# Gated linear recurrence with a maxout feed-forward: a new order of all steps and PSUM rooms, 45 words in column quarters, and the second group's decay sum by an adding transfer

## The chip, the cores and the metric

One core of one Trainium2 chip. The metric is the device time in microseconds of one execution. The kernel before took 555.67 us (median of 3 runs, 555.03 to 556.41).

## What is computed

The reference, cut to what matters (B, H, S, D = 4, 8, 768, 48; 3072 tokens, d_model 384, d_ff 768):

```python
mag = np.sqrt(a_re * a_re + a_im * a_im)
scale = np.minimum(mag, 0.999) / (mag + 1e-06)
a_re_n, a_im_n = (a_re * scale, a_im * scale)
for t in range(S):
    new_re = ar * S_re - ai * S_im          # ar, ai: a_re_n, a_im_n at t
    new_im = ar * S_im + ai * S_re
    kv = np.einsum('bhd,bhe->bhde', k[:, :, t], v[:, :, t])
    S_re, S_im = (new_re + kv, new_im)
    y[:, :, t] = np.einsum('bhd,bhde->bhe', q[:, :, t], S_re)
x = y.transpose(0, 2, 1, 3).reshape(B * S, H * D)
h = np.maximum(np.maximum(x @ w1, x @ w2), x @ w3)
return (h @ w_out).astype(np.float32)
```

A complex decay per head and channel multiplies a state in each of the 768 steps, the state takes k times v and is read by q; the result of all heads goes through three products, their maximum, and one more product. The weights arrive as float64.

## The kernel before, in words

The recurrence is made of blocks of 128 steps. A **group** (number 0 to 11 after the colon of a word) holds one block for two batch entries, x and y; two runs of six groups cover four entries. The decay is taken apart into a size (as a sum of logarithms, tile Ln) and an angle (running sums of turns, cs, then sines). q and k are scaled and turned by those, transposed (tp), and multiplied for scores within a block (A and B, picked into atm by masks); across blocks a state g is carried (dk, and h-steps on it). `y` adds scores times v and q times the state. The feed-forward for a group of 256 tokens: `U` multiplies by w2 and w3 after w1 was subtracted from them (so the third branch folds into wp, from T, M and W steps at the start), the u-steps take the maximum, and P1 to P7 with S1 to S4, r- and o-steps are one level of Strassen's scheme for the last product; Px and Py add the third branch.

Every step is a **word** such as `U01:3` or `Kcx:5`, and `SCHEDULE` lists all words in one order. `run` turns a word into instructions; class `Bound` ties each instruction to the one before it on its engine, so the engines (PE, DVE, ACT, POOL, and SP for loads and stores) each follow the list in their own order and wait only by semaphores. Line 107 is the helper through which all of them go, so every row of the profile carries it, and rows are told apart by their tiles. `SLOTS` says which of four PSUM rooms of two banks each a word's result takes; a room is free when its readers are done. `OTHER` names the words that run on the other engine than usual: copies, magnitudes and casts on DVE and not on ACT, `addw` and `Lnop` on DVE and not as an adding transfer by POOL's queue. `QUARTERS` (empty) names the words whose matmuls are cut.

What the change and the prediction touch:
- `mmf`: a wide matmul (U, P, Px, O, M), 128 by 128 weights, or four of 32 columns each where its word is in `QUARTERS`; `angles` makes `cs` in pieces of 64 columns, or 32.
- `gates`: `pw` adds w and L with two matmuls by the identity into PSUM where the group is under `SUMS`; else `addw` adds L to w in place (`increase`: DVE, or a transfer that adds). `lnw` takes the log of the sum, and the angle follows from it.
- `weight_step`: `Wa` casts the raw weights (tile xhx from w, wo, strassen or xhx), `We` joins both parts on DVE, `Wg` subtracts.
- In the program a matmul of two float32 operands is one instruction; the trace has two for it.

```python
for o in range(0, P, 32) if T["word"] in QUARTERS else ():
    mm(out=out[o:o + 32], lhsT=lhsT[:, o:o + 32], rhs=rhs, **kw)
if T["word"] not in QUARTERS:
    mm(out=out, lhsT=lhsT, rhs=rhs, **kw)
```

Of the kernel before, what the change touches and what calls it, by code (L numbers as in the profile page):

```python
# [29 lines left out]
0624060202264204602604204624604602204600406204240620420460246260246202460246024062624640406204602602  # L30
6402466024240642460246026042064264064240246060206426040260046024240604204060420602640424062420242002
4202
"""

OTHER = set("""
Zf:0 Zg:0 afx:0 relu:1 Qcy:0 addw:2 Lnop:2 Wg8:0 u21y:0 addw:3 relu:4 afx:3 abs:4 Lnop:4 u01:2 xx:3 afy:4 afx:5 addw:6 u01:4 afx:6 afy:6 abs:7 relu:8 Kcy:6 afy:7 afx:7 relu:9 abs:9 u11:7 u01:7 afx:9 Kcx:9 xy:8 u11:8 Kcy:9 afy:10 abs:11 Kcx:10 Qcy:10 Kcy:11 Kcx:11 xy:11 u01:11 u11:11
""".split())

QUARTERS = set("""
""".split())  # L40

ROOMS = {0: "w1", 3: "w2", 6: "wo", 11: "w1", 1: "w2", 9: "H", 10: "S", 2: "H", 4: "S", 5: "H", 7: "S", 8: "H"}
# [927 lines left out]
```

## Time and profile before

| what | value |
|---|---|
| runs, median (lowest to highest) | 555.67 us (555.03 to 556.41) |
| profiled execution, its own time | 555.11 us |
| its span, first to last instruction | 553.4 us |
| busy: PE, DVE, ACT, POOL | 524.8, 470.8, 369.7, 70.7 us |
| mean granted clock of PE | 0.988 |
| matmul records, weight loads | 10086, 10086 |
| PE's longest wait (F for DVE's Ln) | 9.1 us, once |
| ACT's table loads | 49, 62.9 us |
| share of DMA engines, 0 to 62.5 us and 80 to 540 us | 0.91 and 0.34 |

The page gives the busy time of each engine, then its share in 40 slices of 13.8 us. A table by stage gives busy time in chosen stretches. Groups of instructions have columns line, engine, operation, tiles (out<-in), shapes, count, busy us and mean ns of one, and idle time before them with what ended it. A matmul's shape stands as rows * columns of the weights. The chain of waits lists start, length and what ran. A matmul's duration of some 200 to 500 ns is its passage through the array; many overlap, so steps from one start to the next, not durations, show what one costs.

### The profile page before, as it was taken

The page shows a single profiled execution, that of the slowest core. Times are in us where ns is not written, and L with a number is a line of the kernel's source. Part 1 is how long each engine was busy: PE and PEld are TensorE (multiplying, and loading weights), DVE is VectorE, ACT ScalarE, POOL GpSimd, SP SyncE. Part 2 cuts the span into 40 slices and gives each one's busy share as a digit, 9 for nine tenths or more (in the row PEclk, how much of TensorE's full clock was granted, in tenths as well). Part 3 has the DMA queues.
Part 4 walks back from the last instruction along what each step waited for, and adds up shares of the span by engine and source line. Part 5 has one row for each costly group of instructions (what it writes and reads, how often), then busy time and mean ns, then how long its engine had stood idle before and what let it go on. Part 6 is the DMA issues. An engine that isn't in the chain of part 4 may idle for free.

```text
span 553.4 us, 22672 instructions
## 1 busy us (share of the span) xinstructions
PE 524.8 (95%) x10086; PEld 449.1 (81%) x10086; DVE 470.8 (85%) x728; ACT 369.7 (67%) x653; POOL 70.7 (13%) x117
## 2 busy tenths in 40 slices
PE   3579899999999999999999999999999999999996
PEld 1355687788888888888988988988988988898985
DVE  4788889999999997999988888999999998887432
ACT  7999997877867787868776768786637835520100
POOL 8314130030020020000210200120020020000000
PEclk9879899999999999999999999999999999999999
DMA  8999774262516332324453256342350153000000
GB/s 227 272 236 195 168 125 80 51 128 63 108 40 122 69 67 53 61 44 89 80 111 58 35 102 129 64 91 52 67 123 18 32 107 70 3 31 2 31 1 28
DMA packets 141953, 47.50 MB, mean 86 GB/s; under 512 B 130464, under 2 KB 139040, under 8 KB 141856
## 3 DMA queue, kind: packets, MB, share of 16 engines
q1 hardware_dynamic: 136272, 37.76, 31.3%
q0 software_dynamic: 5584, 8.30, 9.0%
q8 instruction: 79, 1.29, 0.9%
q14 instruction: 18, 0.15, 0.1%
HBM read 33.02 MB, written 4.72 MB: 68 GB/s over the span
## 4 chain that ended last, share of the span: by engine, by line
PE 84%; ACT 5%; SPq 5%; DVE 2%; DMA 2%; issue 1%; DVEq 0%; ACTq 0%
PE up L107 33%; PE op L107 24%; PE y L107 7%; PE A L107 5%; SPq L107 5%; PE tp L107 4%; PE dk L107 3%; PE cs L107 3%; PE sums L107 2%; PE F L107 2%; PE B L107 1%; DMA ar<-in_a_re_dram 1%; ACT L L107 1%; ACT L107 1%; DMA ai<-in_a_im_dram 1%
## 5 line engine op out<-in xcount | busy, mean ns | idle before, releaser
L107 PE MATMUL up<-xhx,w 128*128 128x256 f32 x792 | 177.0, 382 | 0.1
L107 PEld LDWEIGHTS up<-xhx,w 128*128 128x128 f32 x792 | 148.9, 190 | 21.2 <-PE B L107 0.3
L107 ACT ACT_TABLE_LOAD x49 | 62.9, 1283 | 1.6 <-PEq L954 0.8
L107 ACT COPY atm<-B 32x128 f32<-32x128 f32 x96 | 24.5, 255 | 36.6 <-DVE atm L107 19.1
L107 PE MATMUL op<-wo,xhx 128*128 128x192 f32 (+1 forms) x220 | 48.6, 364 | 0.0
L107 DVE TENSOR_TENSOR Q<-Q,f 112x1024 f32<-112x1024 f32 (+1 forms) x48 | 45.4, 953 | 2.1 <-ACT Q L107 1.2
L107 POOL DMA_DIRECT2D ar<-nf x40 | 34.6, 1304 | 60.5 <-DVE ar L107 49.2
L107 ACT ACTIVATE f<-F 48x232 f32<-48x232 f32 x96 | 34.4, 359 | 10.3 <-PE F L107 6.3
L107 PEld LDWEIGHTS op<-wo,xhx 128*128 128x128 f32 x220 | 36.5, 190 | 4.8 <-issue 0.8
L107 PE MATMUL y<-atm,vb 128*32 128x64 f32 x1152 | 39.3, 222 | 0.1
L107 PE MATMUL y<-QG,g 112*32 112x64 f32 x1408 | 38.1, 219 | 0.3 <-issue 0.3
L107 PEld LDWEIGHTS y<-atm,vb 128*32 128x32 f32 x1152 | 32.5, 110 | 5.4 <-issue 2.9
L107 PEld LDWEIGHTS y<-QG,g 112*32 112x32 f32 x1408 | 34.9, 110 | 0.5 <-issue 0.5
L107 DVE TENSOR_TENSOR ot<-ot,op 128x384 f32<-128x384 f32 (+1 forms) x56 | 25.6, 465 | 10.7 <-PE op L107 6.4
L107 PE MATMUL op<-wo,strassen 128*128 128x192 f32 x176 | 33.0, 331 | 0.0
L107 POOL DMA_DIRECT2D Ln<-e x9 | 8.3, 923 | 192.0 <-ACT e L107 73.7
L107 DVE COPY_PREDICATED atm<-masko,A 128x256 f32<-128x256 uint8 x72 | 31.3, 436 | 1.7
L107 PE MATMUL op<-w,strassen 128*128 128x192 f32 x176 | 32.2, 329 | 0.0
L107 PE MATMUL A<-Q,K 112*32 112x80 f32 x1536 | 31.6, 234 | 0.2 <-DVE Q L107 0.2
L107 PEld LDWEIGHTS A<-Q,K 112*32 112x32 f32 x1536 | 27.3, 110 | 3.0 <-issue 1.6
L107 ACT COPY Q<-tp 112x1024 f32<-112x1024 f32 x22 | 22.3, 1015 | 10.7 <-PE tp L107 10.6
L107 PEld LDWEIGHTS op<-wo,strassen 128*128 128x128 f32 x176 | 28.8, 190 | 0.8
(149 smaller groups left out, 1071.5 us busy)
## 6 DMA issues: line engine op xcount, KB each, us to landing
ar<-in_a_re_dram SPq DMA_DIRECT2D x24, 192.0 KB, 3.4
ai<-in_a_im_dram SPq DMA_DIRECT2D x24, 192.0 KB, 3.4
q<-in_q_dram SPq DMA_DIRECT2D x96, 48.0 KB, 2.8
k<-in_k_dram SPq DMA_DIRECT2D x96, 48.0 KB, 2.7
vb<-in_v_dram SPq DMA_DIRECT2D x96, 48.0 KB, 2.6
...
```

The lines of the kernel that those rows point to most:

```text
L107: ins = f(*a, **kw)
```

## The change

All of `SCHEDULE` is in another order, and `SLOTS` with it. `OTHER` changes: among others the casts Wa3, Wa0, Wa9, Wa10, Wa1 and Wa5 go to DVE. `QUARTERS` holds 45 words: 13 `cs`, five `U`, seventeen `P`, ten `Px` or `Py`, nearly all of groups 8 to 11. Counted along PE's order, the matmuls change between tile shapes 159 times (189 before), which makes 160 runs of one shape. `SUMS` goes from 2 to 1: group 1's `pw` goes, and its `addw`, which is not in `OTHER`, is an adding transfer.

```diff
 SCHEDULE = """
-Lrx:0 sqr0:0 Lix:0 sqi0:0 add0:0 lnL0:0 expe0:0 expw0:0 lne0:0 relu0:0 Z0:0 Z1:0 WL0:0 Liy:0 Wa0:0 sqi1:0 Zf:0 Lry:0 ...
+Z1:0 Lrx:0 sqr0:0 Lix:0 sqi0:0 add0:0 lnL0:0 expe0:0 xor0:0 expw0:0 lne0:0 Lry:0 Zg:0 Z0:0 Liy:0 Liy:1 relu0:0 Lnop0:0
...
 QUARTERS = set("""
+csy:1 csy:3 csx:3 csx:4 csy:4 Py:2 Py:3 csy:6 csx:6 csx:7 Px:5 Py:5 csy:9 csy:10 P1:8 P7:8 csx:10 P5:8 P6:8 Px:8 U12:9
+P7:9 csy:11 csx:11 Py:9 P4:9 U11:10 U01:10 U02:10 U12:10 Py:10 Px:10 P2:10 P5:10 P7:10 P6:10 Px:11 P4:10 Py:11 P5:11
+P1:11 P4:11 P6:11 P2:11 P3:11
 """.split())
...
-    SUMS, ADDS = 2, 1
+    SUMS, ADDS = 1, 1
...
             if g >= SUMS:
-                increase(w, L)
+                increase(w, L if g >= ADDS else e)
```

Three places, as the programs have them (the line number is that of the helper in each file).

ACT in the start, before: the casts of two weight blocks (xhx<-w_125, xhx<-w_126), between them the f-steps of the y half of group 0, and the log of pw (L<-pw), which holds the decay sum of group 1.

```order
L107 ACTIVATE xhx<-w_125 128x768
L107 ACTIVATE e<-e 128x768
L107 ACTIVATE f_99<-F 48x4x58
L107 ACTIVATE En_118<-sums 128x384
L107 ACTIVATE f_99<-F 48x4x58
L107 ACTIVATE Ek_114<-sums 128x384
L107 ACTIVATE f_99<-F 48x4x58
L107 COPY g_87<-dk 112x2x4x48
L107 ACTIVATE f_99<-F 48x4x58
L107 ACTIVATE xhx<-w_126 128x768
L107 ACTIVATE L<-pw 128x768
L107 ACTIVATE L<-L 128x768
```

The same place after, from the magnitude that feeds the adding transfer (L<-ar) to the log of its sum.

```order
L210 ACTIVATE L<-ar 128x768
L210 COPY vb_85<-wt 128x768
L210 ACTIVATE Eq_116<-sums 128x384
L210 COPY vb_86<-wt 128x768
L210 ACTIVATE Ek_114<-sums 128x384
L210 ACTIVATE e<-e 128x768
L210 ACTIVATE t_106<-nf_108 128x384
L210 ACTIVATE xhx<-w_125 128x768
L210 ACTIVATE f_99<-F 48x4x58 x4
L210 ACTIVATE L<-w 128x768
L210 ACTIVATE L<-L 128x768
```

The log reads w and no longer pw, and one cast of two is left here.

DVE in the start, before: from the second sum of squares to the first products of group 0's angle.

```order
L107 ISA L<-L,e 128x384
L107 SCALAR_TENSOR_TENSOR ai<-ar,ai 128x384
L107 TENSOR_SCALAR ar<-ar 128x384
L107 SCALAR_TENSOR_TENSOR w_124<-w_125,xhx 128x3x256
L107 SCALAR_TENSOR_TENSOR Ln_111<-L,e 128x384
L107 SCALAR_TENSOR_TENSOR ai<-ar,ai 128x384
L107 SCALAR_TENSOR_TENSOR w_124<-w_126,xhx 128x3x256
L107 TENSOR_TENSOR w<-pw,L 128x384
```

The same place after.

```order
L210 ISA L<-L,e 128x384
L210 TENSOR_SCALAR ar<-ar 128x384
L210 TENSOR_SCALAR xhx<-w_126 128x768
L210 SCALAR_TENSOR_TENSOR w_124<-w_126,xhx 128x3x256
L210 SCALAR_TENSOR_TENSOR Ln_111<-L,e 128x384
L210 SCALAR_TENSOR_TENSOR ai<-ar,ai 128x384
L210 TENSOR_TENSOR w<-pw,L 128x384
L210 TENSOR_SCALAR xhx<-w_125 128x768
```

The casts (TENSOR_SCALAR xhx<-w) now stand in DVE's order, and two more of them follow within its next thirty rows.

PE at the end of the program, before: the last four U and the products of group 11 (op is the result's room; strassen holds the S sums, w_124 and wo the factors).

```order
L107 MATMUL up<-xhx,w_126 128x256 x9
L107 MATMUL up<-xhx,w_125 128x256 x18
L107 MATMUL up<-xhx,w_126 128x256 x9
L107 MATMUL op<-wo,xhx 128x192 x4
L107 MATMUL op<-wo,xhx 128x384
L107 MATMUL op<-wo,xhx 128x192 x4
L107 MATMUL op<-wo,strassen 128x192 x4
L107 MATMUL op<-w_124,strassen 128x192 x4
L107 MATMUL op<-wo,xhx 128x384
L107 MATMUL op<-wo,strassen 128x192 x4
L107 MATMUL op<-w_124,strassen 128x192 x4
L107 MATMUL op<-w_124,xhx 128x192 x4
```

The same place after.

```order
L210 MATMUL up<-xhx,w_125 128x256 x9
L210 MATMUL up<-xhx,w_126 128x256 x9
L210 MATMUL op<-w_124,strassen 128x192 x4
L210 MATMUL op<-wo,xhx 32x384 x4
L210 MATMUL op<-wo,strassen 32x192 x16
L210 MATMUL op<-wo,xhx 32x192 x16
L210 MATMUL op<-w_124,xhx 32x192 x16
L210 MATMUL op<-w_124,strassen 32x192 x16
L210 MATMUL op<-wo,xhx 32x192 x16
L210 MATMUL op<-wo,strassen 32x192 x16
```

From Py on every product is in quarters (32 columns, four times as many), and the products with the second halves (P2, P3) have moved behind P4.

More of the change, by code (lines that the diff above doesn't have):

```diff
@@ new lines @@
+WL9:0 f2x:0 Wa9:0 WL10:0 add:1 nfy:0 We9:0 Lqy:0 WL1:0 Qcx:0 Q1x:0 Q2x:0 lnL:1 expe:1 tpkx:0 Kcx:0 expw:1 relu:1
+sumsy:0 Eny:0 T2:0 t2:0 Wa10:0 kEnx:0 Ax:0 g0x:0 abs:1 addw:1 T0:0 t0:0 T1:0 QBx:0 g1x:0 g2x:0 g3x:0 Lvx:0 dkx:0
+WL11:0 Eqy:0 mqy:0 t1:0 Eky:0 lne:1 afy:0 Wa11:0 Fy:0 Lix:2 M0:0 KBx:0 We10:0 QGx:0 We11:0 half:1 f1y:0 Wa1:0 f2y:0
+f0y:0 Cdy:0 f3y:0 lnw:1 expL:1 Lky:0 mky:0 We1:0 mulai:1 h1x:0 h2x:0 mulw:1 Bx:0 b0x:0 h3x:0 b1x:0 M1:0 stt:1 Lry:2
+sby:0 say:0 uky:0 WL4:0 Wa4:0 atan:1 yx:0 xx:0 Liy:2 uqy:0 tpky:0 Kcy:0 kEny:0 We4:0 tpqy:0 Lnop:1 sqi:2 Cdx:0 Qcy:0
@@ new lines @@
+turn:1 Q1y:0 Q2y:0 WL2:0 Lrx:2 sqr:2 add:2 Wa2:0 Lvy:0 Lkx:1 We2:0 QBy:0 M2:0 csx:1 lnL:2 tx:1 Ay:0 m0:0 nfx:1 g0y:0
+expe:2 m1:0 relu:2 Fx:1 dky:0 h1y:0 Wg1:0 g1y:0 KBy:0 g2y:0 g3y:0 QGy:0 csy:1 ty:1 nfy:1 WL7:0 expw:2 U01x:0 Wa7:0
+Lqx:1 WL5:0 By:0 xor:2 u01x:0 Wg4:0 Z2:0 Wg2:0 abs:2 We7:0 half:2 b0y:0 b1y:0 sumsx:1 Ekx:1 Enx:1 Eqx:1 addw:2 lnw:2
+expL:2 Cdx:1 yy:0 xy:0 Wa5:0 We5:0 WL8:0 f1x:1 U11x:0 U01y:0 f0x:1 u11x:0 f3x:1 h2y:0 f2x:1 mulw:2 mulai:2 h3y:0 stt:2
+afy:1 atan:2 sby:1 Lqy:1 Lvx:1 afx:1 Liy:3 U11y:0 U02y:0 Wg7:0 Cdy:1 turn:2 mqx:1 mkx:1 Lix:3 Lky:1 Lvx:2 u01y:0
@@ new lines @@
+b0x:1 b1x:1 Ay:1 afy:2 yx:1 kEny:1 say:2 Lvy:2 Lry:3 Lix:4 Dy:0 Lrx:3 g0y:1 g1y:1 xor:3 sqr:3 add:3 g2y:1 Lvy:1 Enx:2
+lnL:3 expw:3 Eqx:2 xx:1 g3y:1 KBy:1 relu:3 expe:3 abs:3 Ox:0 ox:0 ukx:2 QGy:1 mqx:2 uqx:2 By:1 b0y:1 b1y:1 dky:1
+sumsy:2 h1y:1 h2y:1 h0x:2 Eqy:2 mqy:2 Eky:2 Eny:2 yy:1 xy:1 addw:3 uqy:2 J1:0 h3y:1 Lky:2 tpkx:2 tpqx:2 Qcx:2 lnw:3
+expL:3 lne:3 U11:1 Kcx:2 Lvy:3 u11:1 Q1x:2 mky:2 uky:2 tpky:2 tpqy:2 Q2x:2 Liy:4 Ax:2 kEnx:2 half:3 QGx:2 Qcy:2 mulw:3
+mulai:3 stt:3 KBx:2 QBx:2 Fy:2 f2y:2 f3y:2 f0y:2 g0x:2 g1x:2 U01:1 u01:1 Lkx:3 Cdy:2 sqi:4 g2x:2 Kcy:2 f1y:2 Q1y:2
@@ new lines @@
+atan:3 Q2y:2 Lry:4 Lqx:3 Lvx:3 Lrx:4 Cdx:2 turn:3 Lrx:5 g3x:2 kEny:2 U02:1 u02:1 Bx:2 b1x:2 b0x:2 Ay:2 g0y:2 dkx:2
+h1x:2 g1y:2 h2x:2 Lnop:3 sumsy:3 sqr:4 add:4 g2y:2 Eky:3 Eqy:3 Eny:3 h3x:2 KBy:2 QBy:2 U12:1 u12:1 lnL:4 relu:4 expe:4
+csy:3 csx:3 g3y:2 By:2 b0y:2 tx:3 b1y:2 yx:2 nfx:3 dky:2 expw:4 S3:1 abs:4 addw:4 S1:1 P7:1 P5:1 h0y:2 S2:1 h1y:2 P1:1
+J2:0 P6:1 afx:3 h2y:2 QGy:2 h3y:2 ty:3 xx:2 nfy:3 afy:3 xor:4 J4:0 yy:2 Lqy:3 Liy:5 Lix:5 xy:2 sbx:3 lnw:4 Dx:0 r1:1
+Fx:3 expL:4 mulw:4 f1x:3 r6:1 r75:1 r57:1 S4:1 half:4 sax:3 mqy:3 say:3 sby:3 f2x:3 lne:4 uqy:3 sumsx:3 Eqx:3 Lry:5
@@ new lines @@
+lne:5 relu:5 P7:2 Px:2 P2:2 P5:2 P6:2 expw:5 ty:4 sax:4 abs:5 addw:5 Lvx:5 P1:2 KBy:3 QGy:3 nfy:4 g1y:3 g2y:3 g3y:3
+Lkx:4 mkx:4 QBy:3 Py:2 By:3 mqx:4 uqx:4 half:5 Cdy:4 S4:2 dky:3 h1y:3 ukx:4 h2y:3 P4:2 sby:4 r1:2 r6:2 r75:2 P3:2
+r57:2 ox:2 afy:4 oy:2 say:4 b1y:3 b0y:3 yy:3 xy:3 lnw:5 tpqx:4 Qcx:4 tpkx:4 h3y:3 Fx:4 f0x:4 sumsy:4 expL:5 Fy:4 f1y:4
+Kcx:4 f2y:4 f2x:4 mulai:5 kEnx:4 Eqy:4 mulw:5 stt:5 U01:3 f0y:4 f3x:4 f1x:4 Q2x:4 KBx:4 Q1x:4 QBx:4 atan:5 h0x:4 Eny:4
+u01:3 U11:3 f3y:4 h0y:4 Lvx:4 Lqy:4 Dx:2 QGx:4 Liy:6 Lry:6 Lix:6 Lnop:5 Lrx:6 Eky:4 sqi:6 sqr:6 add:6 Lvy:5 xor:6
@@ new lines @@
+u11:3 lnL:6 Lqx:5 Bx:4 Ax:4 Cdx:4 mky:4 mqy:4 Lkx:5 expe:6 lne:6 g0x:4 g1x:4 uqy:4 turn:5 g2x:4 g3x:4 b1x:4 b0x:4
+uky:4 U02:3 u02:3 U12:3 u12:3 tpqy:4 tpky:4 kEny:4 Qcy:4 Kcy:4 dkx:4 sumsx:5 h1x:4 Enx:5 h2x:4 h3x:4 Q2y:4 sumsy:5
+Eky:5 Ekx:5 Eqx:5 Lqy:5 csy:5 ty:5 nfy:5 Eny:5 Eqy:5 csx:5 tx:5 Lry:7 Lrx:7 dky:4 expw:6 Fx:5 f0x:5 Px:3 P2:3 Q1y:4
+S3:3 h1y:4 QBy:4 S1:3 f3x:5 f2x:5 f1x:5 nfx:5 h2y:4 h3y:4 KBy:4 Liy:7 mqy:5 mqx:5 relu:6 abs:6 sbx:5 Ay:4 g0y:4 g1y:4
+g2y:4 yx:4 Py:3 addw:6 xx:4 afx:5 g3y:4 By:4 b0y:4 sax:5 uqx:5 Lix:7 Lky:5 Dy:2 Lqx:6 lnw:6 P5:3 P1:3 P7:3 S2:3 S4:3
@@ new lines @@
+QGy:4 P4:3 P3:3 r1:3 expL:6 mulai:6 mulw:6 tpqx:5 mkx:5 b1y:4 Qcx:5 QBx:5 half:6 yy:4 stt:6 P6:3 r6:3 r75:3 mky:5
+r57:3 xy:4 Q1x:5 afy:5 say:5 Lnop:6 sby:5 sqr:7 Q2x:5 ox:3 uqy:5 ukx:5 oy:3 U11:4 uky:5 Lky:6 Dx:3 u11:4 atan:6 turn:6
+sqi:7 U01:4 u01:4 tpkx:5 tpky:5 tpqy:5 Kcx:5 Qcy:5 Fy:5 f3y:5 kEnx:5 xor:7 add:7 Ax:5 KBx:5 g0x:5 f2y:5 f1y:5 Liy:8
+g1x:5 QGx:5 g2x:5 lnL:7 relu:7 f0y:5 g3x:5 Q1y:5 Kcy:5 Lqy:6 expe:7 lne:7 Lnop:7 h0x:5 U02:4 u02:4 Q2y:5 U12:4 csy:6
+Bx:5 S3:4 csx:6 u12:4 ty:6 nfy:6 b0x:5 b1x:5 expw:7 abs:7 dkx:5 sumsx:6 tx:6 Eqx:6 S1:4 h1x:5 S2:4 Lvx:6 addw:7 lnw:7
@@ new lines @@
+kEnx:6 Q2x:6 U11:5 csy:7 u11:5 ty:7 nfy:7 Ax:6 csx:7 tx:7 dkx:6 nfx:7 Fy:6 f3y:6 f2y:6 Lqx:7 Lvy:7 g0x:6 g1x:6 g2x:6
+f1y:6 QGx:6 QBx:6 afx:7 h1x:6 h2x:6 h3x:6 g3x:6 relu:8 U02:5 lne:8 u02:5 f0y:6 expw:8 abs:8 xor:8 sbx:7 U12:5 KBx:6
+Fx:7 dky:6 h1y:6 u12:5 addw:8 lnw:8 S1:5 S2:5 Q2y:6 Lix:9 f2x:7 f1x:7 sumsx:7 Ekx:7 Enx:7 half:8 S3:5 Eqx:7 f3x:7
+h2y:6 h3y:6 afy:7 P1:5 P6:5 Q1y:6 P5:5 Lnop:8 S4:5 P7:5 f0x:7 Lkx:7 Lrx:9 mkx:7 Bx:6 QBy:6 Ay:6 Px:5 KBy:6 r1:5 r6:5
+b1x:6 b0x:6 Lry:9 sqr:9 r75:5 r57:5 g0y:6 g1y:6 g2y:6 Py:5 yx:6 g3y:6 QGy:6 By:6 expL:8 sax:7 P2:5 Cdx:7 P4:5 P3:5
@@ new lines @@
+b0y:6 xx:6 mqx:7 uqx:7 ukx:7 Lkx:8 b1y:6 yy:6 xy:6 mulw:8 tpqx:7 tpkx:7 h0x:7 ox:5 mulai:8 sby:7 say:7 Kcx:7 oy:5
+U11:6 u11:6 stt:8 Fy:7 kEnx:7 dkx:7 sumsy:7 Eky:7 Eqy:7 Qcx:7 Q2x:7 f1y:7 f2y:7 f0y:7 Q1x:7 QGx:7 QBx:7 h1x:7 h2x:7
+mqy:7 uqy:7 mky:7 Cdy:7 Eny:7 KBx:7 uky:7 h3x:7 sqi:9 atan:8 Lqy:8 U01:6 u01:6 turn:8 f3y:7 Lrx:10 xor:9 U02:6 u02:6
+tpqy:7 Qcy:7 tpky:7 Kcy:7 add:9 lnL:9 Ax:7 Q2y:7 g0x:7 g1x:7 kEny:7 g2x:7 g3x:7 Bx:7 b1x:7 QBy:7 Q1y:7 U12:6 u12:6
+S1:6 S2:6 b0x:7 csx:8 csy:8 tx:8 expe:9 lne:9 ty:8 nfy:8 expw:9 relu:9 Lnop:9 nfx:8 Ay:7 g0y:7 g1y:7 g2y:7 h0y:7 yx:7
@@ new lines @@
+xx:7 afy:8 abs:9 half:9 Lvy:8 addw:9 Cdx:8 lnw:9 expL:9 Lix:10 P5:6 Py:6 Px:6 P1:6 P2:6 Liy:10 Lky:8 Lry:10 say:8
+sqr:10 afx:8 sby:8 S3:6 P7:6 KBy:7 By:7 g3y:7 QGy:7 mulw:9 mulai:9 dky:7 h1y:7 stt:9 S4:6 sax:8 P4:6 P6:6 h2y:7 Dy:5
+Lvx:8 Dx:5 r1:6 r6:6 atan:9 Cdy:8 b0y:7 P3:6 b1y:7 yy:7 sqi:10 Lix:11 r75:6 h3y:7 ox:6 r57:6 oy:6 xy:7 xor:10 add:10
+sbx:8 Fx:8 f2x:8 f3x:8 f1x:8 sumsx:8 Eqx:8 Lqx:8 mqx:8 uqx:8 sumsy:8 Eqy:8 Enx:8 Eky:8 mqy:8 mky:8 Eny:8 f0x:8 Ekx:8
+lnL:10 U11:7 mkx:8 uky:8 ukx:8 turn:9 expe:10 lne:10 Lkx:9 uqy:8 Lqy:9 u11:7 U12:7 u12:7 tpkx:8 tpqx:8 tpqy:8 Qcx:8
@@ new lines @@
+nfx:10 g1y:9 g2y:9 Bx:9 P5:8 QBy:9 g3y:9 b1x:9 KBy:9 P6:8 S4:8 Px:8 b0x:9 yx:9 xx:9 expe:11 By:9 relu:11 QGy:9 xor:11
+afy:10 b1y:9 expw:11 abs:11 b0y:9 r1:8 Dy:7 h0y:9 r6:8 P2:8 Py:8 P4:8 P3:8 sby:10 afx:10 say:10 sbx:10 r75:8 addw:11
+sax:10 dky:9 sumsx:10 Eqx:10 lnw:11 ox:8 r57:8 h1y:9 h2y:9 yy:9 oy:8 h3y:9 Dy:8 Fx:10 f2x:10 sumsy:10 Eny:10 Eqy:10
+Ekx:10 f0x:10 xy:9 mqx:10 uqx:10 f3x:10 mkx:10 ukx:10 expL:11 Eky:10 half:11 mulai:11 Enx:10 U01:9 u01:9 lne:11 Lky:10
+mky:10 U02:9 f1x:10 uky:10 h0x:10 mqy:10 uqy:10 u02:9 Lky:11 Lkx:11 tpqx:10 Qcx:10 tpkx:10 tpky:10 tpqy:10 Kcy:10
```

56 lines of the change are left out of this document (50 added, 6 removed).

## Prediction, made before the change was run

> **What bounds the kernel now.** I read the page first: busy shares and slices.
>
> ```profile
> PE 524.8 (95%) x10086; PEld 449.1 (81%) x10086; DVE 470.8 (85%) x728; ACT 369.7 (67%) x653; POOL 70.7 (13%) x117
> PE   3579899999999999999999999999999999999996
> PEclk9879899999999999999999999999999999999999
> ```
>
> TensorE (PE) is busy 95% of the span, and what it lacks lies in the first five slices, where its granted clock is low too. So there are two stages: a start in which PE waits, and a long rest in which its own work sets the time. The table by stage gives the border.
>
> ```profile
> core 0: us, PE busy (x) PEld busy (x) DVE busy (x) ACT busy (x) POOL busy (x), PEclk, DMA share, GB/s
> 0.00:62.50 62.50, 41.77 (x582) 27.28 (x582) 45.13 (x73) 57.52 (x99) 24.16 (x62) 0.89 0.91 225
> 62.50:80.00 17.50, 15.34 (x293) 14.15 (x290) 15.51 (x25) 16.78 (x29) 7.32 (x8) 1.00 0.72 135
> 80.00:540.00 460.00, 459.12 (x9169) 399.90 (x9169) 406.71 (x625) 295.13 (x526) 39.23 (x47) 1.00 0.34 67
> 540.00:553.40 13.40, 8.58 (x50) 7.72 (x48) 3.39 (x8) 0.32 (x1) 0.00 (x0) 1.00 0.09 29
> ...
> 120.00:160.00 40.00, 39.89 (x859) 34.75 (x859) 38.57 (x60) 29.84 (x52) 4.00 (x5) 1.00 0.44 85
> ```
>
> From 80 to 540 us PE is busy 459.12 of 460: what is taken off its work there comes off the time one for one. Up to 62.5 us ACT is busy 57.52 of 62.5, idle 5.0 us in all, and DVE only 45.13: the start is ACT's. The border is the first `up` matmul, at 62.55 us in the chain of waits.
>
> ```profile
> 62.55 1.61 PE up L107 x12
> ...
> 122.92 4.08 PE up L107 x18
> ...
> 212.78 1.24 PE A L107 x64
> ...
> 219.63 1.45 PE cs L107 x16
> ...
> 287.36 11.85 PE up L107 x54
> ...
> 417.16 7.97 PE up L107 x36
> ```
>
> These rows price PE's work (columns: start, us, instructions). From x18 to x54 are 36 matmuls in 7.77 us: 0.216 us each at 256 columns, and the x36 row lies on that line. 18 of them make 3.89, so a run of them costs 4.08 - 3.89 = **0.19 us extra**, once, for going into the full 128*128 shape and out of it. With small shapes several tiles run side by side: A has 64 instructions of 80 columns in a 128*32 shape; four at a time at 80/256 of 0.216 is 16 x 0.0675 = 1.08 us, measured 1.24. cs (two side by side, 192 columns) is 8 x 0.162 = 1.30, measured 1.45. So a run in a small shape costs some **0.15 us extra**.
>
> **The change, part by part.**
>
> *Behind the first up.* A tile shape is 64 or 128 rows by 32, 64 or 128 columns. In the program's order I counted the places where one matmul's differs from the next one's: 189 before and 159 after; behind the first up 170 and 139. Of those 31, 9 go into 128*128: 9 x 0.19 + 22 x 0.15 = 5.0 us less. No matmul behind that point is dropped; with every one at the steps above, PE's work there is 470.4 us before and 465.3 after: **-5.1 us**. Ends: 0.1 us a change (what A would leave if its four tiles overlapped a little worse) gives -3.1; 0.3 gives -9.3.
>
> *The quarters.* 32 words of wide matmuls (five U, seventeen P, ten Px or Py) are cut into four 32-column pieces each; 13 cs words go from 64 to 32 columns, which is A's shape. The wide words hold 5 x 18 x 0.216 + 17 x 8 x 0.162 + 10 x 2 x 0.323 = 48 us of PE (0.323 by 384/256 of 0.216). The trace has no such piece of 192 or 256 columns. Its nearest row is A, where four tiles side by side ran at full rate but for the 0.16 that I count as the change of shape. I take 0 for the quarters. Ends: 0.16 on 1.08, 15%, would be +7 us if all of it grew with the columns; below, -1 us (pieces load a quarter of the weights when a shape begins).
>
> *The start.* I summed, along each engine's order, what it must have done before the first up can run, each instruction at the mean of its kind.
>
> ```profile
> L107 ACT ACTIVATE xhx<-w 128x768 f16<-128x768 bf16 x4 | 4.2, 1059 | 0.0
> L107 DVE TENSOR_SCALAR xhx<-up 128x768 f32<-128x768 f32 x7 | 6.7, 957 | 11.5 <-PE up L107 11.5
> L107 DVE TENSOR_SCALAR Ln<-L 128x768 f32<-128x768 f32 x4 | 2.2, 553 | 0.0
> ```
>
> ACT: 58.3 us in 98 instructions before (57.52 by the table, so the sum holds), **49.5 in 85 after**. Five of the weight casts, 1.06 us each, go to DVE; second-half exps and copies of the next group move behind. DVE: 43.2 before, **50.5 after**. A cast on DVE isn't in the trace; it lies between 0.55 and 0.96 (the rows above, both 128x768), I take 0.9, and 0.55 would leave DVE at 48.8. PE must do 30.7 us before that point instead of 32.9; that holds the removed pw of group 1, 8 matmuls of 384 columns, 8 x 0.323 = 2.6 us, and this gives nothing of its own, because PE waits there anyway.
>
> With ACT's 5.0 us of idling of before, 49.5 becomes 54.5. But DVE is now as full, and its idling has to be found.
>
> ```profile
> L107 ACT ACT_TABLE_LOAD x49 | 62.9, 1283 | 1.6 <-PEq L954 0.8
> ...
> L107 ACT ACTIVATE CS<-nf 128x384 f32<-128x384 f32 x24 | 12.3, 515 | 0.1
> ...
> L107 ACT ACTIVATE L<-L 128x384 f32<-128x384 f32 x6 | 3.1, 521 | 0.9 <-DVE L L107 0.8
> ...
> L107 DVE TENSOR_TENSOR uk<-CS,k 128x768 f32<-128x768 f32 x24 | 22.9, 953 | 0.2
> L107 DVE SCALAR_TENSOR_TENSOR nf<-t,cs 128x384 f32<-128x384 f32 x24 | 13.2, 551 | 4.4 <-ACT t L107 4.3
> ```
>
> Before the first transposes ACT has 18.9 and DVE 19.3 us to do. I followed the rows there by hand: ACT steps of 0.52, two table loads of 1.28, the first loads waited for as before, then PE cs, ACT t, DVE nf, the sines, DVE uk and uq at 0.95, each after the other. That ends near 24.8 us, so DVE has idled 5.5 by then. 50.5 + 5.5 is 56.0. I add 1 us for two engines that wait on each other with no room on either: **first up at 57.0 instead of 62.5, -5.5 us**. Ends: 54.5 (-8.0), and 62.5 (nothing won).
>
> *The adding transfer.* It takes the place of the pw matmuls; ACT's log of the sum waits for it.
>
> ```profile
> L107 POOL DMA_DIRECT2D Ln<-e x9: 837/877/1167, 37.8 to 434.4; - x9
> DMA to landing us min/median/max: 3.9/4.3/8.4
> ...
> L107 ACT ACTIVATE f<-F 48x232 f32<-48x232 f32 x96 | 34.4, 359 | 10.3 <-PE F L107 6.3 <-DVE g L107 2.3 <-DVE QG L107 0.2
> L107 ACT ACTIVATE Ek<-sums 128x384 f32<-128x384 f32 x24 | 11.6, 488 | 0.3 <-PE sums L107 0.2
> L107 ACT ACTIVATE e<-e 128x768 f32<-128x768 f32 x11 | 9.3, 842 | 0.1
> L107 ACT ACTIVATE t<-nf 128x384 f32<-128x384 f32 x14 | 7.2, 515 | 1.9 <-DVE nf L107 1.9
> L107 ACT COPY vb<-wt 128x768 f32<-128x768 f32 x2 | 1.5, 791 | 0.0
> ```
>
> The first two rows are the Ln transfers' (min, median, max), which carry the same 384 KB. Between the abs that feeds the new transfer and the log, ACT has two wt copies, two exps, an lne, a magnitude, a cast and four f's: 2 x 0.79 + 2 x 0.49 + 0.84 + 0.52 + 1.06 + 4 x 0.36 = 6.4 us. POOL's issue (0.88) and a median landing hide in that; one of 8.4 would not: 0.9 + 8.4 - 6.4 = 2.9 us of ACT. Behind that log in ACT's queue stands the rest of group 1's angles, and PE's cs of group 1 waits for those. Part of the 1 us above is for it, and 2.9 is within the ends.
>
> *The end.*
>
> ```profile
> 545.55 1.46 PE L107 MATMUL op<-w,strassen 128*128 128x192 f32 x8
> 547.05 1.41 DVE L107 TENSOR_TENSOR ot<-ot,op 128x384 f32<-128x384 f32 x3 [2.50 <-PE op L107]
> 548.25 1.57 PE L107 MATMUL op<-w,xhx 128*128 128x192 f32 x8 [1.23 <-DVE ot L107]
> 549.85 0.62 DVE L107 TENSOR_TENSOR ot<-ot,op 128x192 f32<-128x192 f32 x2 [1.39 <-PE op L107]
> ```
>
> Before, the last product waits 1.23 us for DVE's ot sums. After, P2 and P3 come last and those sums lie beside them, but ox (0.55) now stands between the last matmul and oy: -1.23 + 0.55 = **-0.7 us**; ends -1.2 and +0.6.
>
> *The sum:* 553.4 - 5.1 - 5.5 - 0.7 = 542.1 of span. The profiled execution took 555.11 with 1.7 around its span: 543.8. The runs' median, 555.67, is 0.56 above it: **544.4**.
>
> **The rivals.**
>
> *DVE takes ACT's place, and the start wins nothing.* For it: DVE's sum stays beside PE's for long; where PE has 120 us of work behind it, DVE needs 141 us after (132 before). I expect PE there at about 150, and DVE would have to be busy 94%. Against it: DVE was busy 38.57 of 40 between 120 and 160, 96%, without holding PE up. At 90% it gets there at 157, and the win at the start is gone: 544.4 + 5.5 = about **550**.
>
> *The quarters' weights don't hide, and it gets slower.* 492 quartered products are 984 weight loads, where the full shape had 246.
>
> ```profile
> L107 PEld LDWEIGHTS up<-xhx,w 128*128 128x128 f32 x792 | 148.9, 190 | 21.2 <-PE B L107 0.3 <-ACT K L107 0.3 <-DVE ar L107 0.3
> ...
> L107 PEld LDWEIGHTS A<-Q,K 112*32 112x32 f32 x1536 | 27.3, 110 | 3.0 <-issue 1.6 <-PE y L107 0.3 <-ACT K L107 0.3
> L107 PEld LDWEIGHTS y<-QG,g 112*32 112x32 f32 x1408 | 34.9, 110 | 0.5 <-issue 0.5
> ```
>
> A small load has 27.3/1536 = 0.018 us of PEld's time to itself, y's 0.025. If these stood before their matmuls and not beside them, the 984 would add 17.5 to 24.4 us: **562 to 569**. It decides from 13 ns a load, or from 27% on the 48 us. Against it speaks A's row: 64 such loads leave no room for themselves in 1.24 us.
>
> The Trainium skill, page "TensorE: Matmul & The Clock Gate", section "Part 3: Packing small matmuls", says that a weight load overlaps a running matmul only when their row groups differ; quarters use all rows, so by that rule each load would be exposed. By the same page's load time, columns over 1.2 GHz, the estimate would be 27 ns a load, 26 us in all. The trace speaks against the rule: full-row matmuls of up follow each other every 0.216 us with their loads (190 ns mean) hidden, and A's 64 did too.
>
> *It wins more.* The shape changes between the small words could cost 0.3 us, since no row has them alone: -9.3 in place of -5.1, **540**. Against it: cs's row leaves 0.15.
>
> **How the numbers follow.** Forecast 0.62, with its own range 540 to 548; DVE's place 0.19; quarters, whole or in good part, 0.11; more 0.08. For 8 in 10 the range leaves out the lower half of "more" and the quarters' case: **539 to 553**. About 0.3% (1.7 us) is what a measurement of this kernel can tell from no change. Faster by over that 0.85 (all but the quarters and the worst of DVE's case), within it 0.05, slower 0.10.
>
> **What would show it.** First up at 55 to 59 us; ACT and DVE both busy over 85% until then. Rows of `up` in 128*32 form: a run of 72 pieces at 18 x 0.216 = 3.9 us, not 5 or more. Some 31 fewer changes with the same steps. The wait of ACT's L for the w transfer under 3 us. The last matmuls without a wait for ot. I would be wrong if PE shows waits for DVE beyond 80 us of more than a few us, if the transfers of the start (DMA share 0.91 now) come later than the sums need them, or if a room in PSUM is freed too late, which the sums here can't see.

## Result, and the profile after

| | before | after |
|---|---|---|
| runs beside each other, median (lowest to highest) | 555.53 us (555.03 to 556.41) | 549.66 us (548.59 to 551.66) |
| profiled execution, its span | 555.11, 553.4 us | 548.59, 546.8 us |
| PE busy, matmul records | 524.8 us, 10086 | 517.7 us, 10920 |
| first `up` starts at | 62.55 us | 59.05 us |

The ratio is 0.9897, 95% interval 0.9863 to 0.993: the change makes the kernel 1.0% faster, 5.9 us, where 11.3 were forecast. Its sign and most of its parts came as predicted, its size is about half. The ratios here and below leave out runs over 1.5% longer than the fastest of the same kernel, and of `whole` one such run is the one that was profiled.

Page after, busy times, PE's slices and its clock, and the row of the queue that brings PE its instructions:

```profile
PE 517.7 (95%) x10920; PEld 438.8 (80%) x10920; DVE 478.0 (87%) x748; ACT 368.7 (67%) x639; POOL 71.5 (13%) x116
PE   4498799999999999999999999999899999999996
PEclk9789899999999999999999999999999999999999
q8 instruction: 86, 1.41, 1.1%
```

Table by stage after (us, then busy us and count of PE, PEld, DVE, ACT and POOL, PE's clock, DMA share, GB/s):

```profile
0.00:62.50 62.50, 42.76 (x718) 29.05 (x722) 52.71 (x86) 53.58 (x92) 26.15 (x62) 0.89 0.96 234
62.50:80.00 17.50, 15.95 (x245) 14.16 (x238) 16.11 (x25) 16.47 (x35) 5.91 (x7) 1.00 0.64 132
80.00:540.00 460.00, 456.58 (x9915) 393.92 (x9918) 406.85 (x632) 298.41 (x514) 39.46 (x47) 1.00 0.34 66
```

PE's busy time fell by 7.1 us; the counted steps of the prediction give 7.3 for both stages (470.4 + 32.9 = 503.3 before, 465.3 + 30.7 = 496.0 after). ACT and DVE are level in the start, 53.58 and 52.71. But behind 80 us PE is idle 3.4 of 460 us, where it was 0.9. Chain of waits after (start, us):

```profile
32.23 5.79 DMA w<-L
...
59.05 2.54 PE up L210 x12
...
480.53 3.88 PE up L210 x72
...
486.35 4.02 PE up L210 x72
```

The quarters run at full rate: 72 pieces take 3.88 to 4.02 us, as 18 whole ones did. The first `up` comes at 59.05, 2.05 us later than the forecast 57.0, and its 12 matmuls take 2.54 us, where the same 12 took 1.61 before. The adding transfer is on the chain above, but ACT's log of the sum waits for it by 0.16 us only (ACT, timeline):

```profile
38.10 0.84 ACT L210 ACTIVATE L<-w 128x768 f32<-128x768 f32 x1 [0.16 <-DMA w<-L]
```

The end (timeline) has no wait for ot any more; the last sums follow the last product at once:

```profile
540.95 1.48 PE L210 MATMUL op<-wo,strassen 128*32 128x192 f32 x32
542.50 1.08 DVE L210 TENSOR_TENSOR ot<-ot,op 128x384 f32<-128x384 f32 x3 [0.92 <-PE op L210]
```

What is new stands in PE's waits, in rows that name no engine ("issue": the profile shows nothing that PE waited for). After, and before:

```profile
PE dk L210 <- issue: 2.0, 1, 2.0
PE y L210 <- issue: 1.8, 2, 1.0
PE F L210 <- issue: 1.3, 1, 1.3
...
PE op L210 <- issue: 0.4, 1, 0.4
```

```profile
PE up L107 <- issue: 0.5, 1, 0.5
PE y L107 <- issue: 0.3, 1, 0.3
```

F's has a cause: its room in PSUM is freed by DVE's nf, which ends at 53.77. So has one of y's two (0.84 us, at 63.78), for ACT copies its atm until 63.68:

```profile
62.64 1.04 ACT L210 COPY atm<-B 32x128 f32<-32x128 f32 x4
```

The others have none. The largest, in PE's timeline after:

```profile
51.21 1.31 PE L210 MATMUL A<-Q,K 112*32 112x80 f32 x64
53.87 0.55 PE L210 MATMUL F<-cuts,Ln 64*48 64x29 f32 x31 [1.35 <-issue]
...
54.26 0.49 PE L210 MATMUL dk<-vb,uk 64*64 64x48 f32 x17
56.75 0.90 PE L210 MATMUL dk<-vb,uk 64*48 64x48 f32 x46 [2.00 <-issue]
57.59 1.46 PE L210 MATMUL cs<-w,upto 128*32 128x192 f32 x16
58.98 2.61 PE L210 MATMUL up<-ot,w 128*128 128x128 f32 x12
```

PE stops in the middle of dk, between matmuls of one tile whose inputs were all there. This stop is the 2 us by which the first `up` is late.

**Theory "supply".** The queue row says 86 packets and 1.41 MB: 16 KB each. PE's own order has 21987 places (10920 weight loads, 10920 matmuls and 147 semaphore steps; a matmul of the program has two passes, each a weight load and a matmul), and 21987 / 86 is 256. So PE's instructions come in blocks of 256, and PE stops where a block isn't there yet. Worked out from the trace's matmul and packet records, all places where PE lost 0.35 us or more within 2 us of a packet's end and near the end of a block (the stop is the gap between two starts, less 0.1):

```
after:  place, block x 256 + rest   stop us   packet of instructions   PE goes on
         1217   4 x 256 + 193         2.1       54.45 to  55.41           56.75
         3521  13 x 256 + 193         0.35     109.51 to 110.63          111.91
         6849  26 x 256 + 193         0.9      189.53 to 190.46          191.81
        14530  56 x 256 + 194         0.65     380.76 to 381.76          383.18
        14785  57 x 256 + 193         1.1      386.62 to 387.56          388.81
before:  1474   5 x 256 + 194         0.7       68.65 to  69.61           70.92
         2753  10 x 256 + 193         0.5       98.18 to  99.53          100.83
```

Every stop lies 193 or 194 places into a block, counted from the first place of the trace, and PE goes on 1.2 to 1.5 us after a packet's end: 5.1 us in all after, 1.1 before. In all fourteen traces of this document the packets are exactly as many as the places of this kind that PE passes (86 after, 79 before), so this is where one block ends and another is asked for; why the rest is 193 the traces don't show. One of the stops stands in PE's waits under another name: that of 191.81 is put down to DVE's ot (0.8 us), which had ended 0.35 us earlier, and with the borders moved (shift30) the same word has no wait.

**Rival "DVE"**: the prediction's own, that DVE has taken ACT's place; the stops would be waits whose cause the trace doesn't name. **Rival "quarters"**: they cost PE more than the changes of shape that they save.

### The profile page after: what moved, and what is told of

The parts are those of the page before. It is cut to its first block, busy times and chain, and to the rows that moved or that the text cites. A ratio compares the mean times of both kernels' runs of the same rounds, so it can differ in the third digit from the quotient of the medians.

```text
span 546.8 us, 24317 instructions
## 1 busy us (share of the span) xinstructions
PE 517.7 (95%) x10920; PEld 438.8 (80%) x10920; DVE 478.0 (87%) x748; ACT 368.7 (67%) x639; POOL 71.5 (13%) x116
## 3 DMA queue, kind: packets, MB, share of 16 engines
q8 instruction: 86, 1.41, 1.1%
## 4 chain that ended last, share of the span: by engine, by line
PE 81%; DVE 5%; issue 4%; DMA 3%; ACT 3%; SPq 2%; POOL 1%; DVEq 0%; ACTq 0%; POOLq 0%
PE up L210 33%; PE op L210 21%; PE y L210 6%; PE A L210 5%; PE tp L210 4%; PE dk L210 3%; PE cs L210 3%; PE sums L210 2%; SPq L210 2%; PE F L210 1%; PE B L210 1%; DMA k<-in_k_dram 1%; DMA ar<-nf 1%; DMA w<-L 1%; DVE w L210 1%
## 5 line engine op out<-in xcount | busy, mean ns | idle before, releaser
L210 PE MATMUL up<-xhx,w 128*128 128x256 f32 (+1 forms) x1062 | 178.6, 382 | 0.1
L210 PEld LDWEIGHTS up<-xhx,w 128*128 128x128 f32 (+1 forms) x1062 | 144.4, 163 | 25.6 <-issue 1.4
L210 PE MATMUL op<-wo,xhx 128*128 128x192 f32 (+3 forms) x376 | 49.3, 373 | 0.0
L210 DVE TENSOR_TENSOR Q<-Q,f 112x512 f32<-112x512 f32 (+1 forms) x48 | 45.1, 953 | 1.6 <-ACT Q L210 1.5
L210 PEld LDWEIGHTS op<-wo,xhx 128*32 128x32 f32 (+1 forms) x376 | 34.7, 146 | 5.4 <-issue 1.6
L210 PE MATMUL op<-w,strassen 128*32 128x192 f32 (+1 forms) x320 | 32.8, 328 | 0.4 <-issue 0.4
L210 PE MATMUL op<-wo,strassen 128*128 128x192 f32 (+1 forms) x272 | 32.9, 329 | 0.0
L210 ACT ACTIVATE xhx<-up 128x768 f32<-128x768 f32 x17 | 13.7, 805 | 25.9 <-PE up L210 25.8
L210 PEld LDWEIGHTS op<-w,strassen 128*32 128x32 f32 (+1 forms) x320 | 28.0, 142 | 1.9 <-issue 0.7
L210 POOL DMA_DIRECT2D w<-L x7 | 6.2, 890 | 178.2 <-ACT L L210 99.9
```

Of the source, the lines that this page charges most:

```text
L210: ins = f(*a, **kw)
```

## The experiments

Ratios are to the kernel before on the same chip; the change stands at 0.9897. Span, first `up` and stops are those of one profiled execution each. "Stops" are counted as in the list above, those over 0.25 us at 193 or 194 places into a block.

| run | ratio, 95% interval | span us | first up us | stops, us |
|---|---|---|---|---|
| before | 1 | 553.4 | 62.5 | 1.1 |
| after | 0.9897 (0.9863 to 0.993) | 546.8 | 59.0 | 5.1 |
| shift30 | 1.0232 (1.018 to 1.0283) | 567.4 | 61.6 | 16.6 |
| shift60 | 1.0039 (1.0014 to 1.0064) | 556.0 | 66.7 | 4.2 |
| shift90 | 1.042 (1.0374 to 1.0466) | 582.8 | 70.8 | 20.9 |
| whole | 1.0137 (1.0071 to 1.0204) | 569.1 | 59.7 | 15.4 |
| after16 | 0.9982 (0.9966 to 0.9997) | 551.8 | 61.0 | 8.4 |
| after64 | 1.0169 (1.0141 to 1.0197) | 563.0 | 57.0 | 18.2 |
| before64 | 1.0325 (1.0304 to 1.0347) | 571.0 | 63.3 | 16.6 |
| casts_act | 1.005 (1.003 to 1.007) | 556.6 | 61.5 | 5.8 |
| csy_first | 0.9898 (0.9875 to 0.9921) | 548.6 | 59.0 | 3.1 |
| dk_first | 0.9888 (0.9861 to 0.9915) | 546.8 | 58.4 | 2.5 |
| add_dve | 0.9921 (0.9897 to 0.9945) | 549.2 | 61.1 | 4.7 |
| sums_only | 1.016 (1.0129 to 1.019) | 562.9 | 66.5 | 7.5 |

### Tiny matmuls that move the borders of the blocks

In the word pw of the first group, behind its own matmuls (30, 60 or 90 of them; nothing reads them):

```
+                if lo == 0:
+                    for i in range(30):
+                        mm(out=ps[0:32, 0, 384 + 8 * (i % 16):392 + 8 * (i % 16)], lhsT=ident[0:32, 0:32], rhs=ident[0:32, 0:8], start=True, stop=True)
```

> The changed kernel with 30 tiny extra matmuls (32x8, results unused) behind the first pw, where PE is idle; nothing else differs. In the changed kernel's trace TensorE stops at 54.5, 190.8, 382.4 and 387.6 us (2.1, 0.9, 0.7 and 1.1 us) with no late input; counted in PE's own instruction order (weight load and matmul of each pass, and semaphore steps) the four places are 1217, 6849, 14530 and 14785, which all lie 193 or 194 behind a multiple of 256, and in each case a 16 KB packet of instructions ended 1.3 to 1.7 us earlier. Theory 'supply' (PE runs out of instructions, which come in blocks of 256): the extra instructions move every later border 60 or 120 places forward in the order, so all four stops leave their words, and stops that come up elsewhere stand at the same place in a block; the sum of such stops may be anything from 0.5 to 6 us, so the time is 544 to 551. Rival 'DVE' (the start and the rooms in PSUM are held by DVE): the same four waits at the same words, time within 1 us of the changed kernel (548.6 to 549.7). Both: no cost of the 30 matmuls themselves over 0.3 us.

> As shift30 with 60 tiny matmuls: borders moved by 120 or 240 places of 256. 'Supply': the four stops of the changed kernel gone from their words (at 240 of 256 some may be left some 16 places on), others at 194 behind a border; time 544 to 551, and different from shift30's by as much as the stops differ. 'DVE': the same waits, time within 1 us of the changed kernel.

> As shift30 with 90 tiny matmuls: borders moved by 180 or 360 (104 of 256) places. 'Supply': the four stops gone from their words, others at 194 behind a border; time 544 to 551. 'DVE': the same waits, time within 1 us of the changed kernel.

Each tiny matmul has two passes, so the moves are 120, 240 and 360 places. Not as expected by either theory: 30 tiny matmuls make the kernel 3.4% slower than the change, 569.2 us in the median, and all three runs lie outside "544 to 551" (shift60 557.4, shift90 579.7). One part was my placing: they stand on the start's chain, 3.4, 6.6 and 9.8 us, not under 0.3:

```profile
10.99 3.37 PE L210 MATMUL pw<-ident 32*32 32x8 f32 x60
```

But shift60 has twice the extra matmuls of shift30 and is almost 12 us faster. The stops tell why: 16.6 us, then 4.2 (240 is 16 short of a whole block, so the borders are almost back), then 20.9. The stops of the changed kernel have left their words in shift30 (at one of them, op, 0.35 of 0.65 us is left), and 18 others stand 193 or 194 places into a block. The gaps that have another cause stay with their words: one of 0.64 us before A, at 167.0 in the changed kernel, is 0.64 in shift30, shift60 and shift90 too, each time at another place of a block. "DVE" has no place for this; "supply" has, though I had put its price far too low.

Next the same with 4 or 16 tiny matmuls behind the second pw, where PE waits 4 us anyway (`if g == 0 and lo > 0`), in the changed kernel and in the one before:

> The changed kernel with 4 tiny extra matmuls behind the second pw (PE is idle there for 4.1 us; 8 records of 0.054 us by the run with 30 of them are 0.4 us, hidden): every border of PE's blocks of 256 moves by 16 places and nothing else. Taking from the changed kernel's trace how long PE took for each stretch of 256 places (and 16 more that it reads ahead), and letting no block be ready sooner than 3.3 us after the one before it is begun, the missing time adds up to 2.9 us where the borders are now (measured 5.1), and 1.3 us with the borders 16 further. 'Supply': 1 to 4 us of stops are left, 546 to 549.5, a little faster than the changed kernel. 'DVE': 549 to 550, the same waits as the changed kernel.

> As after16 with 16 tiny matmuls: borders moved by 64 places, 32 records of 0.054 us, 1.7 us, hidden in the 4.1 us. By the same sum the stops are 12 us (11 to 17 by how far PE reads ahead). 'Supply': 7 to 12 us slower than the changed kernel, 556 to 562, with some ten to fifteen stops 194 places behind a multiple of 256. Rival 'the tiny matmuls themselves cost' (which stood on the critical chain in the runs with 30 to 90 of them): under 2 us slower, no new stops.

> The kernel before with the same 16 tiny matmuls at the same place, borders moved by 64 places. In its own trace the stops add up to 1.1 us (two, at 70.9 and 100.8); by the sum over its stretches of 256 places they are 2.4 us as it stands, and 12 (10 to 18) with borders 64 further. 'Supply': 8 to 16 us slower than before, 563 to 571. Rival 'only the changed kernel's quarters and bunched small matmuls run into it': under 2 us slower.

after64 and before64 came as "supply" says, a little over its ranges: 563.7 and 572.9 us in the median. PE's waits of before64, where the kernel before has 0.8 us of such rows:

```profile
PE B L107 <- issue: 3.6, 3, 1.3
PE A L107 <- issue: 3.2, 3, 1.6
PE up L107 <- issue: 2.8, 3, 1.0
PE cs L107 <- issue: 1.3, 1, 1.3
PE dk L107 <- issue: 1.0, 1, 1.0
```

Of its 17.6 us of longer span 15.5 are stops. So the supply is nothing that the quarters or the new order brought: 16 tiny matmuls, 1.2 us of PE in front of a wait (the first `up` comes 0.8 us later), cost the old kernel 3.3%, nearly all of it because they move each border by 64 places. And after64 shows the start without its stop: the packet for that border came at 48.88 there, 5.6 us sooner than in the changed kernel:

```profile
54.44 0.55 PE L210 MATMUL F<-cuts,Ln 64*48 64x29 f32 x31 [1.11 <-issue]
...
54.83 1.11 PE L210 MATMUL dk<-vb,uk 64*64 64x48 f32 x63
55.86 0.86 PE L210 MATMUL cs<-w,upto 128*32 128x192 f32 x16
56.98 1.24 PE L210 MATMUL up<-ot,w 128*128 128x128 f32 x9 [0.26 <-PE cs L210]
```

dk runs through, and the first `up` starts at 56.98: the forecast's 57.0.

after16 is a miss. My sum over stretches gave fewer stops than before the move, and there were more, 8.4 us; the run is 4 us slower than the change. The stops stand where they should, but which borders stop is not to be had from PE's pace alone. How soon a packet comes varies too: at the stops of all fourteen traces PE goes on between 2.2 and 10.4 us after it passed the border before, 3.7 in the median, where the sum took 3.3 throughout. That PE reads 16 places ahead, as the sum has it, is shown by no run.

The Trainium skill, page "Runtime: NRT & Kernel Launch", section "Instruction fetch mechanics", says that instructions arrive in 16 KiB blocks of 256 through a DMA queue of the engine's own, and that crossing a block's end is mostly hidden, because the sequencer issues more slowly than blocks are filled. The blocks and the queue agree with this trace (86 packets for 21987 places). By count the hiding agrees too, for 81 of 86 borders cost nothing; but the other five cost 5.1 us here, and 20 borders cost 20.9 us in shift90. The reason given does not hold where PE runs its smallest tiles: 64 matmuls of A take 1.31 us, so 256 places would pass in 2.6 us, and a block takes 2.9 (in the changed kernel a packet starts 0.6 us behind PE's passing the border before, in the median, lasts 1.0, and PE goes on 1.3 later).

### The quarters

The list QUARTERS emptied, nothing else:

> The changed kernel without its quarters: all 45 words in whole tiles as before. 193 changes of tile shape instead of 159, and 1684 fewer places in PE's instruction order (79.3 blocks of 256 instead of 85.9). By the steps of the prediction (0.15 to 0.19 us a change) PE's work grows by 34 x 0.15 to 0.19 = 5.1 to 6.5 us, so the span goes from 546.8 to 552 to 553. 'Supply': the first quartered word stands at about 97 us, so the stop at 54.5 stays as it is and those at 382 and 387 move or go: 551 to 553. A rival 'quarters cost' (their weight loads or their number of instructions slow PE by more than the changes of shape save): 549 or less.

The runs spread from 559.0 to 571.5 us, and the ratio, 1.0137, lies some 13 us above the change's. The rival "quarters" asked for 549 or less, and no run comes near it. The theory's number, 551 to 553 of span, is missed as well, for the fewer places (20303) also move the borders: the profile has 15.4 us of stops, 10.3 more than after. With 34 changes of shape at 0.15 to 0.19 (5.1 to 6.5) that would be 15.4 to 16.8 us, but the profiled execution (569.1) is one of the longest, and how the 13 us are made up isn't settled. Nor is the first quartered word at 97 us, as the expectation has it: csy:1 runs at 57.6, still behind the first stop. So the run does not measure the quarters by themselves; the rows of 72 pieces above do.

### The start: ACT or DVE

```
 OTHER = set("""
-Zg:0 Z0:0 Wa3:0 Wa0:0 Zf:0 afx:0 Wa9:0 relu:1 Wa10:0 Wa1:0 tx:1 addw:2 Wa5:0 afy:1 Wg7:0 u21y:0 Wg8:0 xx:1 relu:3
+Zg:0 Z0:0 Zf:0 afx:0 relu:1 tx:1 addw:2 afy:1 Wg7:0 u21y:0 Wg8:0 xx:1 relu:3 ...
...
```

> The changed kernel with the six weight casts (blocks 3, 0, 9, 10, 1, 5) back on ACT, five of them ahead of the first up; PE's order and so the borders stay as they are. By the prediction's sums ACT then has 49.5 + 5 x 1.06 = 54.8 us to do ahead of the first up and DVE 50.5 - 4.5 = 46. If ACT's share sets the start, the first up comes 1 to 4 us later than 59.0 and the time is 550.5 to 554. If DVE had taken ACT's place ('DVE'), the first up comes earlier than 59 and the time is 546 to 549.

```profile
0.00:62.50 62.50, 40.57 (x671) 26.64 (x672) 47.78 (x79) 55.67 (x94) 25.94 (x62) 0.89 0.97 234
```

With PE's order untouched, moving the casts back makes DVE idle (47.78 busy) and ACT fuller (55.67), the first `up` 2.5 us later, and the kernel 7.8 us slower in the median: ACT's load still counts in the start, and "DVE" falls. The cost is above the 550.5 to 554 expected. Stops are only 0.7 us more; but the place of PE's order that the changed kernel reaches at 126.2 us comes at 134.9 here, 8.7 us later, so ACT's load is felt well beyond the first `up`.

### The adding transfer

In the changed kernel `addw:1` is put into OTHER, which makes it a DVE addition. In the kernel before `pw:1` becomes `addw:1`, its room goes, and SUMS is 1:

> The changed kernel with the second group's sum added by DVE instead of the adding transfer; PE's order stays. DVE gets one more 128x768 addition of 0.96 us ahead of the first up, and ACT's log no longer waits for a transfer (it waited 0.16 us). If the start is held by ACT and by PE's stop, the time stays within 1 us of the changed kernel: 549 to 550.5. If DVE has become what holds the start, it is 1 us slower or more: 550.6 to 552.

> The kernel before with only the second group's decay sum by the adding transfer (its pw:1 and that word's room are taken out); no other part of the change. PE does 8 matmuls of 0.32 us less at 35 us, where it waits anyway; its order gets 17 places shorter, and by the sum over its stretches the stops stay at 2 to 3 us. The prediction gives this part nothing of its own: 553.5 to 556.5. If PE's work ahead of the first up were worth its time, 552 to 553; if the transfer comes late for ACT's log, 557 to 559.

Without the transfer the changed kernel takes 550.46 us; the intervals overlap with the change's. In its profile the first `up` comes at 61.1, with DVE's nf, and so F, 1.3 us later, as "DVE" would have it; the runs' medians differ by 0.8 us (1.3 by the ratios), which lies on the border between the two expectations. The run leaves it open how much room DVE has left. In the old order the transfer without the rest of the change is a loss of 1.6%, 563.7 us in the median and above all three of its expectations:

```profile
45.85 0.84 ACT L107 ACTIVATE L<-w 128x768 f32<-128x768 f32 x1 [3.97 <-DMA w<-L]
```

```profile
L107 PE MATMUL up<-ot,w x108: 275/275/377, 66.5 to 87.7; 128*128 128x128 f32 x108
```

ACT waits 3.97 us for it, where the new order leaves 0.16; the first `up` comes 4.0 us later; the order is 17 places shorter, which moves the borders, and the stops grow by 6.3. So 3 to 4 of the 9.5 us of longer span are the transfer's own. My "nothing of its own" holds only with the work that the new order puts in front of the log.

### Two words exchanged around the stop at 54.5

```
-expe:2 m1:0 relu:2 Fx:1 dky:0 h1y:0 Wg1:0 g1y:0 KBy:0 g2y:0 g3y:0 QGy:0 csy:1 ty:1 ...
+expe:2 m1:0 relu:2 Fx:1 csy:1 dky:0 h1y:0 Wg1:0 g1y:0 KBy:0 g2y:0 g3y:0 QGy:0 ty:1 ...
```

```
-expe:2 m1:0 relu:2 Fx:1 dky:0 h1y:0 ...
+expe:2 m1:0 relu:2 dky:0 Fx:1 h1y:0 ...
```

> The changed kernel with the word csy:1 (16 quarter matmuls, 1.46 us) put ahead of dky:0 in the order, each with the PSUM room it had; PE's count of instructions is the same, so the later borders stay. In the changed kernel the border falls 18 matmuls into dky:0: PE stops at 54.5, a packet of instructions runs from 54.45 to 55.41, and dk goes on at 56.75; csy:1 follows and the first up starts at 59.0. Here the border falls 2 matmuls into dky:0, behind all of csy:1. If the packet's time stands fast (it waits for the transfers of the start), csy:1 is done inside the old stop, the stop shrinks to under 1 us and the first up starts at 57.5 to 58.2: some 1 us faster, 548 to 549. If the packet is asked for only when PE comes near the border, it comes 1.4 us later as well, and the first up stays at 59: 549.5 to 550.5.

> The changed kernel with dky:0 ahead of Fx:1 (each with its room, same count): dk's room is free at 52.8, F's only at 53.8 when DVE's nf is done, so dk can start at 52.9 and reaches the border at about 53.4. If the packet's time stands fast (54.45), PE stops longer and goes on at 56.75 as before, with F behind it: first up 59.0 to 59.5, no gain or a little slower, 549.5 to 551. If the packet is asked for when PE comes near the border, it comes at about 53.4 and PE goes on at 55.7: first up near 58, 548.5. Rival 'the gap is dk's own' (something that dk waits for which the trace doesn't name): dk waits until 56.75 from its first matmul.

csy_first, PE's timeline:

```profile
54.28 0.56 PE L210 MATMUL F<-cuts,Ln 64*48 64x29 f32 x32 [1.11 <-issue]
54.77 0.86 PE L210 MATMUL cs<-w,upto 128*32 128x192 f32 x16
55.55 0.31 PE L210 MATMUL dk<-vb,uk 64*64 64x48 f32 x3
57.12 1.94 PE L210 MATMUL dk<-vb,uk 64*48 64x48 f32 x61 [1.26 <-issue]
58.99 2.93 PE L210 MATMUL up<-ot,w 128*128 128x128 f32 x12
```

The stop moved to behind the third matmul record of dk, as the place demands, and shrank to 1.4 us. The packet came at 54.85, 0.4 us later than in the changed kernel, as F did: fast in time, not moved with the border. But the 61 matmuls of dk behind it take 1.94 us, not some 1.1, and the 12 of `up` 2.93: the granted clock is 0.65 from 55 to 60 us, and the gain is gone. Median 549.43, no difference from the change.

dk_first has no stop there, and dk runs through, so the gap was nothing of dk's own. It does not try the two expectations on the packet, for in its profile PE's clock was 0.79 and 0.86 from 45 to 55 us, A came 3.0 us later, and the packet (53.35) was in time. But that packet began 1.3 us after PE had passed the border before (52.01), where the changed kernel's began 5.4 us after. At 548.94 us it is the fastest kernel here, by less than can be told from the change.

## Why the prediction was half right

- *Fewer changes of shape, -5.1.* Right as far as sums can tell: 7.1 us less of PE busy, 7.3 by the steps with the dropped pw and the changes ahead of the first `up`. No run takes the changes of shape alone.
- *Quarters at 0.* Right: 72 pieces in 3.88 to 4.02 us. The rival of 562 to 569 is out. The rule of the Trainium skill that the prediction weighs for it, page "TensorE: Matmul & The Clock Gate", section "Part 3: Packing small matmuls", does not hold for these rows: 72 pieces over all rows, with their weight loads, take no longer than 18 whole ones.
- *The start, -5.5.* Mechanism right, ACT relieved and DVE filled: until the first `up` ACT was busy 50.52 us (49.5 forecast) and DVE 50.33 (50.5). The forecast 57.0 is what after64 shows without the stop. The measured 59.05 is that and the stop of 2.1 us. The step that failed is "I add 1 us for two engines that wait on each other": I had looked for what PE might wait for on ACT, DVE, rooms and transfers, and not at PE's own instructions, whose queue the page lists.
- Behind the stop the clock (table by stage after, same columns) costs once more:

```profile
50.00:55.00 5.00, 3.40 (x124) 2.39 (x123) 4.93 (x9) 4.65 (x6) 1.25 (x1) 1.00 1.08 242
55.00:60.00 5.00, 3.25 (x67) 2.39 (x67) 2.23 (x5) 1.39 (x3) 0.00 (x0) 0.77 1.08 259
60.00:70.00 10.00, 8.75 (x176) 7.89 (x176) 8.80 (x14) 9.47 (x20) 5.91 (x7) 0.94 0.32 91
```

  The clock is 0.77 and 0.94 after it, and `up`'s first 12 matmuls take 2.54 us instead of 1.61: 0.9 us. It need not fall: casts_act has the same stop of 2.1 us, its clock stays, and its 12 take 1.60 (table by stage, timeline):

```profile
55.00:60.00 5.00, 1.91 (x112) 1.62 (x107) 4.88 (x10) 3.04 (x5) 1.25 (x1) 1.00 1.14 255
61.48 1.60 PE L207 MATMUL up<-ot,w 128*128 128x128 f32 x12
```

- *Behind the first up.* The term took PE's order to run without a gap, as it had; stops there are 3.0 us after and 1.1 in all before, 1.9 us that the sum lacks.
- *The adding transfer.* Right here (0.16 us of wait), wrong as a general statement (sums_only).
- *The end, -0.7.* Right in kind, 0.3 us too much: the wait of 1.2 us is gone, but from the last product's end to the span's end it is 4.4 us (542.43 to 546.8), where it was 3.6.
- *The sum.* 542.1 of span forecast, 546.8 measured: 2.05 at the start, 0.9 of clock, 1.9 of stops behind and 0.3 at the end add up to 5.1, where 4.7 are missing; the difference of 0.4 isn't accounted for. The median then lies 1.1 us above the profiled execution, not 0.56: 0.5 more.

That the measured time is what the rival "DVE takes ACT's place" gave (about 550) is chance: the first `up` did come 3.5 us earlier, and casts_act shows that ACT's relief is worth having. The range, 539 to 553, was wide enough to hold a loss of 5 us whose causes the sum did not contain.

What stays open: why a packet sometimes starts late. In the changed kernel, csy_first, add_dve, casts_act and after16 that of the first stop began 0.4 to 0.6 us after PE's wait at F had ended, in the changed kernel 5.4 us after PE had passed the border before; the DMA engines were full then (share 1.08). Full queues alone need not do that: they were as full where the packet came sooner, 3.2 us after the border in after64 (share 1.18) and 1.3 us in dk_first (1.10 and 0.97), and in both no wait of F lay between border and packet. That speaks for the wait at F, but no run tries it alone.
